# Five of 64 large stores split into strided transfers meant to relieve one DMA engine

## Chip, cores, metric

One core of a Trainium2 chip. The batches of runs were on different chips (0, 3, 5, 6, 8 and 10 by the record; that of the first pair is not recorded), and each is compared with the kernel before in its own batch. The metric is the device time of one execution in microseconds (us), the median of several runs. Engine names are those of the profile: PE is TensorE, DVE is VectorE, ACT is ScalarE, POOL is GpSimd, SP is SyncE. The profile counts 16 DMA engines for the core and does not number them. Where the texts number engines, the numbers are my names: 7 for the one that the change was to relieve, 15 for a second.

## The reference

Attention of one query row per head, and its gradients, 64 heads (2 x 32), 8192 keys, head size 128, all bf16:

```python
def _fwd_reference(q, k, v):              # q [2,32,1,128], k and v [2,32,8192,128]
    scale = q.shape[-1] ** -0.5
    scores = jnp.einsum("bhqd,bhkd->bhqk", q, k) * scale
    p = _softmax(scores, axis=-1)
    return jnp.einsum("bhqk,bhkd->bhqd", p, v)

def reference(q, k, v, grad_out):
    out, vjp = jax.vjp(_fwd_reference, q, k, v)
    return out, *vjp(grad_out)            # out, dq, dk, dv
```

k and v are read once (268 MB) and dk and dv written once (268 MB); everything else is small.

## The kernel before

The heads are worked on in 32 pairs. A pair's k is one tile of 4 MB in SBUF, 128 partitions of 128 rows of 256 bytes, and its v is another. Six such tiles circulate. The gradient is written over the tile itself, the tile is stored, and then the slot takes the next load:

```python
load_eng = nc.sync
store_eng = nc.gpsimd
pin = tc.keep_in_program_order
# ...
def load(i, w, pieces=(NCH,)):                          # w = 0: k, w = 1: v
    h = pairs_[i]
    t = kvp.tile([P, NT, D], BF16, tag=f"kv{slot_of(i, w)}", name="kvt")   # six slots
    # ...
        pin(load_eng.dma_start(out=t[:, n0:n1, :], in_=src[:, n0:n1, :]))  # L93
# ...
def outer(i, w, c, ends):
    # ... DVE writes the gradient of chunk c over the tile ...
    if c + 1 in ends:                                   # ends is whole: one store per tile
        at = ends.index(c + 1)
        b0, b1 = (ends[at - 1] if at else 0) * CH, (c + 1) * CH
        dst = (dv_v if w else dk_v)[i]
        pin(store_eng.dma_start(out=dst[:, b0:b1, :], in_=h.tile[w][:, b0:b1, :]))   # L446
```

A load of a slot waits for the store of what the slot held. In the trace each store's semaphore gets 16 increments, and the load is issued about 0.1 us after the 16th (at 194.77, 215.03, 235.12 and 255.31 us for stores whose 16th came at 194.7, 214.9, 235.1 and 255.2 us). The program gives the DMAs of the store queue eight semaphores in turn (the trace shows eight, 111 to 118), so a transfer is issued only when the one eight before it has landed.

## Time and profile before

| | before |
|---|---|
| median of 3 runs | 1308.88 us (1304.53 to 1310.17) |
| span of the profiled run, mean TensorE clock | 1310.5 us, 0.923 |
| bytes moved, mean rate | 539.58 MB, 412 GB/s |
| wait of the load queue for stores | 1188.3 us |

The page of the kernel before: span, busy tenths in 40 equal slices, mean rate of each slice, and the transfers by size with their median time from issue to landing.

```profile
span 1310.5 us, 41375 instructions
...
POOL 0000000000000000000000000000000000000000
...
DMA  9999999999999999999999999999999999999968
GB/s 399 429 374 429 427 429 427 429 428 428 427 424 417 429 422 421 413 415 418 414 413 412 411 417 420 413 417 419 403 421 411 421 408 414 425 404 423 414 257 348
DMA packets 19933, 539.58 MB, mean 412 GB/s; under 512 B 2480, under 2 KB 2480, under 8 KB 2992
...
out_dram<-kvt POOLq DMA_DIRECT2D x62, 4096.0 KB, 40.2
```

The DMA engines are busy throughout, and POOL, which issues the stores, has almost nothing to do.

The longest waits of the load queue's sequencer in the kernel before (total us, times, longest us):

```profile
SPq L93 <- DMA out_dram<-kvt: 1188.3, 58, 59.9
```

Nearly every load waits for a store. The same kernel in five stretches (window, length, busy time of PE, PE weight loads, DVE, ACT and POOL, TensorE clock, DMA share, GB/s):

```profile
100.00:300.00 200.00, 186.52 (x3208) 138.71 (x3205) 143.22 (x260) 165.92 (x111) 5.84 (x11) 0.96 1.00 429
300.00:500.00 200.00, 178.81 (x2965) 132.45 (x2965) 131.24 (x240) 152.30 (x100) 5.32 (x10) 0.92 1.00 424
500.00:700.00 200.00, 176.98 (x2906) 130.43 (x2904) 128.14 (x233) 149.38 (x98) 4.78 (x9) 0.91 1.00 415
700.00:900.00 200.00, 178.59 (x2961) 131.92 (x2958) 131.18 (x238) 152.32 (x100) 5.32 (x10) 0.92 1.00 415
900.00:1060.00 160.00, 138.72 (x2276) 102.60 (x2275) 102.56 (x185) 116.89 (x75) 4.25 (x8) 0.90 1.00 415
```

The rate falls from 429 to 415 GB/s while the DMA share stays 1.00. The semaphores hint at why. I take the 16 increments of a store to come from one engine each. That is an inference: the store queue has 1088 packets of 4 bytes for 68 transfers, 16 for each. Some store landings read from the trace, in us:

```
before   1st    12th    13th    16th
       187.7   191.2   191.9   194.7
       205.9   210.7   211.2   214.9     <- the store that the change splits first
       225.5   231.6   232.1   235.1
       243.7   251.0   251.4   255.2
```

From 100 us on, the last increments follow each other every 20.2 us on average. The last increment is about 2 to 3 us behind the first at 100 us, and 16 to 22 us behind it from 320 us on, with a gap of its own behind the fifteenth of mostly 6 to 11 us. I read this as one engine that lags: the others run ahead for the first 300 us, at 429 GB/s, and then wait for it. The profile does not say which engine it is.

The change assumes that the rows of partitions 28-31 and 60-63 are the slow engine's, and that its transfers hand them to other engines.

### The profile page before, as it was taken

What the parts mean: (1) busy time and instruction counts of PE and PEld (TensorE: products, weight loads), DVE (VectorE), ACT (ScalarE), POOL (GpSimd) and SP (SyncE); (2) the same over time, 40 slices, a digit from 0 to 9 for tenths busy, and PEclk for the clock granted to TensorE, in tenths of its full rate; (3) what the DMA queues carried; (4) which work ended last, traced back from release to release, by engine and by line L of the source; (5) the groups of instructions that cost most, each with busy time, mean ns of one, the idle gap of its engine ahead of it and who ended that gap; (6) DMA issues with size and microseconds to landing.
All of it is one profiled execution on the core that took longest, in us unless ns stands there. A gap on an engine that the chain in (4) does not pass through costs nothing.

```text
span 1310.5 us, 41375 instructions
## 1 busy us (share of the span) xinstructions
PE 1147.5 (88%) x19108; PEld 849.1 (65%) x19108; DVE 850.5 (65%) x1551; ACT 984.3 (75%) x641; POOL 37.4 (3%) x76
## 2 busy tenths in 40 slices
PE   5999998898988988989889898898998988888894
PEld 4777766676766666666666676666666666666661
DVE  0677875766766767657676675665766757566666
ACT  5999987876877877778777787777876878777770
POOL 0000000000000000000000000000000000000000
PEclk9999998998989989889898898988988989888896
DMA  9999999999999999999999999999999999999968
GB/s 399 429 374 429 427 429 427 429 428 428 427 424 417 429 422 421 413 415 418 414 413 412 411 417 420 413 417 419 403 421 411 421 408 414 425 404 423 414 257 348
DMA packets 19933, 539.58 MB, mean 412 GB/s; under 512 B 2480, under 2 KB 2480, under 8 KB 2992
## 3 DMA queue, kind: packets, MB, share of 16 engines
q1 hardware_dynamic: 9968, 268.51, 49.5%
q0 software_dynamic: 9792, 268.44, 48.2%
q8 instruction: 149, 2.44, 0.7%
q14 instruction: 24, 0.20, 0.0%
HBM read 268.47 MB, written 268.47 MB: 410 GB/s over the span
## 4 chain that ended last, share of the span: by engine, by line
issue 78%; DMA 14%; PE 3%; POOL 2%; DVE 1%; SPq 0%; POOLq 0%; ACT 0%; DVEq 0%; ACTq 0%
DMA kvt<-in_v_dram 11%; DMA out_dram<-kvt 3%; POOL out_dram L446 2%; PE tp L183 1%; DVE kvt L432 1%; PE acc L376 1%; PE dpw L194 1%; POOLq L446 0%; PE sw L194 0%; ACT ev L185 0%; DVE sel L399 0%; SPq L93 0%; SPq L100 0%; PE sw L222 0%; PE acc L413 0%
## 5 line engine op out<-in xcount | busy, mean ns | idle before, releaser
L185 ACT COPY ev<-tp 128x2048 bf16<-128x2048 bf16 x512 | 954.0, 1865 | 293.6 <-PE tp L183 276.1
L183 PE MATMUL tp<-ident_bf,kvt 128*128 128x128 bf16 x8192 | 585.3, 229 | 127.3 <-DMA kvt<-in_k_dram 76.8
L432 DVE TENSOR_TENSOR kvt<-qb,pair 128x2048 bf16<-128x2048 bf16 x512 | 615.3, 1219 | 49.6 <-PE acc L376 46.7
L183 PEld LDWEIGHTS <-kvt 128*128 128x128 bf16 x8192 | 505.1, 103 | 137.2 <-DMA kvt<-in_k_dram 79.1
L194 PEld LDWEIGHTS <-ev 128*128 128x128 bf16 x8192 | 239.9, 96 | 218.0 <-issue 135.4
L376 PE MATMUL acc<-kvt,E_pad 128*64 128x512 bf16 x1024 | 173.1, 421 | 0.0
L376 PE MATMUL acc<-kvt,dS_pad 128*64 128x512 bf16 x1024 | 169.4, 416 | 1.0 <-DVE dS_pad L362 1.0
L194 PE MATMUL sw<-qdT,ev 128*128 128x2 bf16 x4096 | 142.0, 164 | 2.2 <-ACT ev L185 2.2
L194 PE MATMUL dpw<-qdT,ev 128*128 128x2 bf16 x4096 | 142.2, 164 | 1.0 <-ACT ev L185 1.0
L270 DVE CUSTOM_DVE_ANT_0 junk<-E_f,dpw 64x128 bf16<-64x128 f32 x64 | 18.3, 285 | 144.1 <-PE dpw L194 143.7
L207 DVE TENSOR_REDUCE mp<-sw 64x1 f32<-64x128 f32 x64 | 18.5, 289 | 108.5 <-PE sw L194 108.1
L446 POOL DMA_DIRECT2D out_dram<-kvt x68 | 36.3, 534 | 1261.7 <-DVE kvt L432 632.9
L399 DVE SCALAR_TENSOR_TENSOR sel<-acc,diag,sel 128x128 f32<-128x128 f32 x192 | 67.3, 351 | 6.8
L376 PEld LDWEIGHTS <-dS_pad 128*64 128x64 bf16 x1024 | 38.2, 112 | 29.4 <-issue 6.3
L376 PEld LDWEIGHTS <-E_pad 128*64 128x64 bf16 x1024 | 37.7, 112 | 26.8 <-issue 6.5
L262 DVE CAST E_pad<-E_f 64x128 bf16<-64x128 f32 x64 | 15.3, 239 | 48.5 <-ACT E_f L252 48.5
L413 PE MATMUL acc<-par,sel 128*128 128x2 f32 x128 | 22.0, 241 | 8.0 <-DVE sel L399 8.0
L176 DVE CAST qb<-dpw 128x128 bf16<-128x128 f32 x64 | 18.2, 284 | 13.4 <-PE dpw L167 13.4
L413 PEld LDWEIGHTS acc<-par,sel 128*128 128x128 f32 x128 | 19.7, 195 | 9.5 <-DVE sel L399 9.5
L340 DVE TENSOR_SCALAR negdelta<-dpw,rl 128x1 f32<-128x1 f32 x32 | 7.0, 218 | 27.0 <-PE dpw L300 27.0
L252 ACT ACTIVATE E_f<-sw,negm 64x128 f32<-64x128 f32 x64 | 23.2, 362 | 1.6
L352 DVE SCALAR_TENSOR_TENSOR dSu<-dpw,negdelta,E_f 64x128 f32<-64x128 f32 x64 | 22.4, 350 | 2.1
(49 smaller groups left out, 230.1 us busy)
## 6 DMA issues: line engine op xcount, KB each, us to landing
out_dram<-kvt POOLq DMA_DIRECT2D x62, 4096.0 KB, 40.2
kvt<-in_v_dram SPq DMA_DIRECT2D x32, 4096.0 KB, 27.8
kvt<-in_k_dram SPq DMA_DIRECT2D x31, 4096.0 KB, 27.9
out_dram<-kvt POOLq DMA_DIRECT2D x3, 2048.0 KB, 8.7
kvt<-in_k_dram SPq DMA_DIRECT2D x1, 2048.0 KB, 11.5
kvt<-in_k_dram SPq DMA_DIRECT2D x2, 512.0 KB, 4.5
kvt<-in_k_dram SPq DMA_DIRECT2D x1, 1024.0 KB, 6.9
out_dram<-kvt POOLq DMA_DIRECT2D x1, 1024.0 KB, 7.6
```

The costliest lines, as they stand in the source:

```text
L183: pin(nc.tensor.transpose(tp[:, t, :], src[:, c * CH + t, :], ident_bf[:]))
L185: pin(nc.scalar.copy(out=ev[:], in_=tp[:]))
L194: nc.tensor.matmul(dst[:, c * CH + t, :], lhsT=ev[:, t, :], rhs=qdT[:, w, GH * i : GH * (i + 1)], start=True, stop=True,)
L207: pin(nc.vector.reduce_max(out=h.mp[hs], in_=h.s[hs, :, g], axis=AX.X))
L252: nc.scalar.activation(out=h.E_f[hs], in_=h.s[hs, :, g], func=ACT.Exp, bias=h.negm[hs], scale=scale, accum_out=h.ld[hs, g : g + 1],)
L270: nc.vector.tensor_tensor_reduce(out=junk[hs], in0=h.E_f[hs], in1=h.dp[hs, :, g], scale=1.0, scalar=0.0, op0=ALU.mult, op1=ALU.add, accum_ ...
L352: nc.vector.scalar_tensor_tensor(out=dSu[hs], in0=h.dp[hs, :, g], scalar=negdelta[hs], in1=h.E_f[hs], op0=ALU.add, op1=ALU.mult,)
L376: nc.tensor.matmul(h.acc[w][g : g + CW, :], lhsT=wts[:, n0 * GH : n0 * GH + CW], rhs=rows[:, n0 : n0 + QT, :].rearrange("p n d -> p (n d)" ...
L399: nc.vector.scalar_tensor_tensor(out=h.sel[:], in0=block, scalar=diag[:, b : b + 1], in1=h.sel[:], op0=ALU.mult, op1=ALU.add,)
L413: nc.tensor.matmul(h.acc[w][:, 0:GH], lhsT=h.sel[:], rhs=par[:], start=True, stop=True)
L432: nc.vector.tensor_tensor(out=h.tile[w][:, n0 : n0 + CH, :].rearrange("p n (e t) -> p n e t", t=2), in0=h.qb[w][:] .rearrange("p (e t) -> ...
L446: pin(store_eng.dma_start(out=dst[:, b0:b1, :], in_=h.tile[w][:, b0:b1, :]))
```

## The change

For the k stores of pairs 3, 9, 15, 21 and 27, write partitions 28-31 and 60-63, but for one row of 256 bytes per partition, in two transfers of their own, and the rest in 24 strided ones. One store becomes these 26 transfers and eight calls with mode `reset_dge_cursor`:

```diff
-            pin(store_eng.dma_start(out=dst[:, b0:b1, :], in_=h.tile[w][:, b0:b1, :]))
+            if w == 0 and i % 6 == 3 and ends is whole:
+                spread(dst, h.tile[w], b0, b0 + NT // 1)
+                b0 += NT // 1
+            if b0 < b1:
+                pin(store_eng.dma_start(out=dst[:, b0:b1, :], in_=h.tile[w][:, b0:b1, :]))
+
+    def spread(dst, t, b0, b1):
+
+        def put(parts, r0, r1, pieces=1, eng=store_eng):
+            pin(
+                eng.dma_start(
+                    out=dst[parts, r0:r1, :],
+                    in_=t[parts, r0:r1, :],
+                    max_dma_last_dim=(r1 - r0) * D * 2 // pieces,
+                )
+            )
+
+        for j in (0, 1, 2, 3, 32, 33, 34, 35):
+            pin(store_eng.inc_swdge_sem([], [], mode="reset_dge_cursor"))
+            put(slice(j, j + 29, 4), b0, b0 + 1, 2)
+            put(slice(64 + j, 64 + j + 29, 4), b0, b1, 2)
+            put(slice(j, j + 25, 4), b0 + 1, b1)
+        for p0 in (28, 60):
+            put(slice(p0, p0 + 4), b0 + 1, b1)
```

Below, "piece" is one of these transfers and "tail" one of the last two, of partitions 28-31 and of 60-63.

## The prediction

> **What bounds the kernel now.** DMA traffic. The page shows 539.58 MB at 412 GB/s; stretches from 100 to 1060 us show a DMA share of 1.00. In the sequencer's own waits, loads wait 1188.3 us for stores to land: six 4 MB tiles circulate, and a load needs its slot's store to have landed [...].
>
> One engine is slower than the other 15. Each DMA's semaphore gets 16 increments[...]. For the stores landing near 74 to 114 us they lie 2 to 3 us apart. From about 320 us the last comes 16 to 22 us after the first, mostly 6 to 11 us after the fifteenth. Stretches show 429 GB/s at 100 to 300 us and 415 from 500 on: fifteen engines first run ahead, then wait for the slow one. Full-rate packets of 32 KB take 1213 ns; 429 GB/s is 1222 ns per packet and engine; the slow engine's landings, 20.14 us per tile (16 packets), are 1259 ns. 37 ns x 1024 packets = 38 us. The others' idle time hides in load packets stretched past 1213 ns (about 20 us per 50 us, summed over 16 engines, after 500 us) and in the last load, which the first engine finishes at 1242 us and the last at 1261.
>
> The profile does not say which engine it is. [...] the change takes it to be 7.
>
> **What the change does.** In the k stores of pairs 3, 9, 15, 21, 27, partitions 28-31 and 60-63 [...] are written by two small transfers [...]. [...] Perfectly balanced: about 1310 - 36 = 1274 us.
>
> **What it costs.** One issue becomes 26, plus 8 resets. POOL issues take 0.53 us each, so some 15 to 20 us per spread store; POOL is 97% free. Worse: stores share eight semaphores, and each transfer waits for the one eight before it. The eighth piece thus waits until the previous whole store has landed, about 20 us; then at most eight pieces (under three rows per engine) are in flight. A store on an idle queue took about 4 us from issue to first packet, so pieces run at half to all of the rate they need. The next store is issued some 15 us late. My estimate: 1.5 to 7.5 us of idle per spread store on the fast engines, giving back 8 to 37 of the 36 us. Compute is unchanged.
>
> **Prediction.** 1288 us, range 1274 to 1308; faster by over 2%: 0.30, within 2%: 0.66, slower: 0.04.
>
> **Signs.** Landings of ordinary stores stay within about 10 us of each other throughout; GB/s stays near 425 after 400 us; stretched load packets become rarer; POOL waits about 20 us for store landings in each spread store, and DMA dips after it. The last load lands near 1240, not 1261.
>
> **What would make it wrong.** The slow engine is 15: time unchanged or worse, landings spread as before. The eight-semaphore window starves the stores more than estimated: dips of 10 us or more, no gain. Or pieces land so quickly that nearly the whole 36 us comes.

The sum came to 1310 - 36 + 8 to 37 = 1282 to 1311 us, of which 1288 was given. The relief, 36 us, is an estimate for perfect balance: the 38 us of excess (37 ns x 1024) less its sixteenth. That the change would bring it was assumed.

## The result, and the profile after

| | before | after |
|---|---|---|
| median | 1308.76 us (4 runs) | 1385.02 us (4 runs, 1382.32 to 1388.35) |
| ratio | | 1.059, 95% interval 1.0556 to 1.0623: slower |
| profiled span, clock | 1310.5 us, 0.923 | 1380.5 us, 0.906 |

A ratio here is the mean time of one kernel's runs over the mean of the other's in the same rounds, so not quite the ratio of the medians quoted.

The page of the kernel after, the same lines:

```profile
span 1380.5 us, 41575 instructions
...
POOL 0000012000001300000022000001300000111000
...
DMA  9999998899999898999999899999998999989888
GB/s 404 426 377 426 430 408 304 365 411 425 423 429 420 305 380 362 416 422 425 425 378 324 373 416 416 428 427 401 312 395 363 415 426 424 426 335 338 359 344 352
DMA packets 24014, 539.61 MB, mean 391 GB/s; under 512 B 6240, under 2 KB 6240, under 8 KB 6752
...
out_dram<-kvt POOLq DMA_DIRECT2D x57, 4096.0 KB, 38.6
...
out_dram<-kvt POOLq DMA_DIRECT2D x40, 256.0 KB, 7.1
out_dram<-kvt POOLq DMA_DIRECT2D x40, 222.2 KB, 6.5
...
out_dram<-kvt POOLq DMA_DIRECT2D x10, 127.0 KB, 16.4
```

The bytes are the same and the rate is lower. There are five dips to 304-335 GB/s, one for each spread store. The last line is the surprise: the ten tails carry 127 KB each and take 16.4 us to land, longer than pieces of twice the size.

The waits of the load queue in the kernel after:

```profile
SPq L93 <- DMA out_dram<-kvt: 1264.9, 65, 59.9
```

This wait grew by 1264.9 - 1188.3 = 76.6 us, and the span of the same two profiled runs by 1380.5 - 1310.5 = 70.0 us (the medians by 76.3 us). The loss lies in late stores.

POOL in the kernel after, around the first spread store (start, length, line, and in brackets its idle time before and what ended it). Line 456 is a piece, line 450 an ordinary store:

```profile
175.58 4.01 POOL L456 DMA_DIRECT2D out_dram<-kvt  x7 [18.39 <-DVE sel L393]
194.83 0.55 POOL L456 DMA_DIRECT2D out_dram<-kvt  x1 [15.25 <-DMA out_dram<-kvt]
197.28 0.54 POOL L456 DMA_DIRECT2D out_dram<-kvt  x1 [1.90 <-DMA out_dram<-kvt]
198.72 0.60 POOL L456 DMA_DIRECT2D out_dram<-kvt  x1 [0.91 <-DMA out_dram<-kvt]
201.09 0.55 POOL L456 DMA_DIRECT2D out_dram<-kvt  x1 [1.77 <-DMA out_dram<-kvt]
203.53 0.54 POOL L456 DMA_DIRECT2D out_dram<-kvt  x1 [1.89 <-DMA out_dram<-kvt]
207.83 0.61 POOL L456 DMA_DIRECT2D out_dram<-kvt  x1 [3.76 <-DMA out_dram<-kvt]
211.65 7.14 POOL L456 DMA_DIRECT2D out_dram<-kvt  x13 [3.21 <-DMA out_dram<-kvt]
218.78 1.11 POOL L450 DMA_DIRECT2D out_dram<-kvt  x2
```

The same stretch in the kernel before:

```profile
173.93 0.53 POOL L446 DMA_DIRECT2D out_dram<-kvt  x1 [17.76 <-DVE sel L393]
193.37 0.53 POOL L446 DMA_DIRECT2D out_dram<-kvt  x1 [18.91 <-DVE kvt L432]
215.29 0.53 POOL L446 DMA_DIRECT2D out_dram<-kvt  x1 [21.38 <-DVE sel L393]
```

Seven pieces are issued at once. The eighth waits 15.25 us, until the previous whole store has landed at 194.5 us, and the next ones come one by one as earlier pieces land (a piece that lands at 197.0 us is followed by an issue at 197.28 us); the last 13 are issued without a wait. The next ordinary store is issued at 218.78 us instead of 193.37 us, 25.4 us late. The prediction said this (with 15 us), and it is not the larger part of the loss. That part is seen in the landings:

```
after    1st    12th    13th    16th
       187.6   191.9   192.1   194.5    the ordinary store before
       ...
       218.7   220.0   220.0   221.2    last of the 24 pieces before the tails
       219.6   221.4   227.7   230.3    tail of partitions 28-31
       219.9   221.6   237.4   239.0    tail of partitions 60-63
       230.1   239.5   250.9   256.2    the next ordinary store
       239.8   257.5   270.7   275.6
       256.9   276.9   290.7   295.6
```

The pieces end at 221.2 us, 6.3 us after the 214.9 us at which the whole store had landed before. Then the tails take another 17.8 us, on four engines going by their four late increments, while twelve of the second tail's 16 are in by 221.6 us, and eleven of the next store's by 232.5 us. The second tail comes after the first, it seems on the same four engines: its four packets start at 227.41, 229.26, 229.44 and 229.89 us, and those of the first end at 227.32, 228.96, 229.37 and 229.82 us. In that next store twelve increments arrive by 239.5 us and the other four from 250.9 us on. Each of the 40 packets of the tails (32512 bytes) took 7.3 to 9.7 us; the median of the other 280 packets of that size was 1.2 us.

The store ends 24.1 us late. The next stores then come every 19.5 us or so, the pace of packets of 1.213 us (16 of them are 19.4 us), as if the four engines worked through their backlog, and eleven stores later 14.7 us of the delay is left (451.3 us against 436.6 us). Each of the five spread stores leaves 13 to 15 us in this way; together they are the 70 us of the profiled runs.

### The profile page after: what moved, and what is told of

It is laid out like the page before. It is cut to its first block, busy times and chain, and to the rows that moved or that the text cites. A ratio compares the mean times of both kernels' runs of the same rounds, so it can differ in the third digit from the quotient of the medians.

```text
span 1380.5 us, 41575 instructions
## 1 busy us (share of the span) xinstructions
PE 1117.3 (81%) x19108; PEld 830.6 (60%) x19108; DVE 851.5 (62%) x1551; ACT 984.2 (71%) x641; POOL 107.1 (8%) x201
## 4 chain that ended last, share of the span: by engine, by line
DMA 45%; issue 29%; PE 17%; POOL 4%; DVE 3%; ACT 2%; SPq 0%; POOLq 0%; ACTq 0%; DVEq 0%
DMA out_dram<-kvt 24%; DMA kvt<-in_v_dram 20%; PE tp L183 8%; PE acc L376 4%; POOL out_dram L456 3%; PE dpw L194 2%; DVE kvt L432 2%; PE sw L194 2%; ACT ev L185 1%; DMA qd_nat<-in_q_dram 1%; POOL out_dram L450 1%; ACT E_f L252 0%; PE sw L222 0%; PE dpw L313 0%; PE dpw L300 0%
## 5 line engine op out<-in xcount | busy, mean ns | idle before, releaser
L183 PE MATMUL tp<-ident_bf,kvt 128*128 128x128 bf16 x8192 | 568.0, 225 | 225.2 <-DMA kvt<-in_v_dram 190.9
L183 PEld LDWEIGHTS <-kvt 128*128 128x128 bf16 x8192 | 489.1, 101 | 234.9 <-DMA kvt<-in_v_dram 192.9
L376 PE MATMUL acc<-kvt,E_pad 128*64 128x512 bf16 x1024 | 163.1, 400 | 0.0
L450 POOL DMA_DIRECT2D out_dram<-kvt x63 | 33.8, 538 | 1019.1 <-DVE sel L393 580.3
L456 POOL DMA_DIRECT2D out_dram<-kvt x130 | 72.3, 560 | 242.5 <-DMA out_dram<-kvt 134.4
## 6 DMA issues: line engine op xcount, KB each, us to landing
out_dram<-kvt POOLq DMA_DIRECT2D x10, 127.0 KB, 16.4
```

What stands on the lines that cost most here:

```text
L183: pin(nc.tensor.transpose(tp[:, t, :], src[:, c * CH + t, :], ident_bf[:]))
L376: nc.tensor.matmul(h.acc[w][g : g + CW, :], lhsT=wts[:, n0 * GH : n0 * GH + CW], rhs=rows[:, n0 : n0 + QT, :].rearrange("p n d -> p (n d)" ...
L456: eng.dma_start(out=dst[parts, r0:r1, :], in_=t[parts, r0:r1, :], max_dma_last_dim=(r1 - r0) * D * 2 // pieces,)
```

## The experiments

The theory after reading the two traces was: the tails cost most of the loss, the eight semaphores the rest, and the relief gave nothing. The rivals were that the relief did come and the pieces cost all the more, and that the engine meant to be relieved was slow but spread stores hid it. Each experiment is an edit of the changed kernel, or of the kernel before where said.

### 1. tail_dropped: the change without its tails (wrong result)

```diff
-        for p0 in (28, 60):
-            put(slice(p0, p0 + 4), b0 + 1, b1)
```

> Wrong result on purpose: in the five spread stores partitions 28-31 and 60-63 are not written (except their first 256 bytes); the other 24 pieces are unchanged. Theory T (the two 4-partition transfers, whose 32.5 KB packets took about 9.2 us instead of 1.2 us, cost the time by holding four engines some 19 us): 1275 to 1300 us, below the kernel before. Theory W (the window of eight semaphores starves the stores while the 24 pieces are issued): 1365 to 1385 us, as the changed kernel. If both matter, the difference to the changed kernel is T's part and the rest W's; each spread store's cost in the changed kernel was 24.6 us (landing of the spread store, 239.0 against 214.9 us).

Measured: 1321.80 us, before in the same batch 1309.60 us, ratio 1.0101 (1.0086 to 1.0116). The two tails, 6% of the bytes of a spread store (254 of 4096 KB), cost 1385.02 - 1321.80 = 63 us, or 12.6 us per spread store.

### 2. home_rows: the same pieces with the tails' rows in them, no tails

```diff
-            put(slice(j, j + 25, 4), b0 + 1, b1)
-        for p0 in (28, 60):
-            put(slice(p0, p0 + 4), b0 + 1, b1)
+            put(slice(j, j + 29, 4), b0 + 1, b1, 2)
```

> The lower pieces take 8 partitions each, [...] the two 4-partition transfers are gone: no relief, no tail, only 24 pieces and 8 resets in five stores. Theory T: 1305 to 1325 us (as before, plus at most 3 us per spread store). Theory W: 1385 us or more, since the relief is lost as well. In both, the ordinary stores away from the spread ones should again land every 20.3 us and not every 19.4 us as in the changed kernel, if it is engine 7 that is slow; if they stay at 19.4 us the relief was not what made them faster.

Measured: 1322.67 us, ratio 1.0111 (1.0084 to 1.0138). Splitting alone costs 13 us, 2.6 us per spread store. This kernel writes all rows, tail_dropped leaves out those of partitions 28-31 and 60-63 in the five stores (but for 256 bytes per partition), and they differ by 0.9 us, inside both intervals. Not having to write these rows is worth nothing that these runs can see.

### 3. tail_four_ports: four-partition transfers that are not neighbours

In home_rows, the groups j = 3 and j = 35 are written by two transfers of four partitions, each four apart:

```diff
+            if j in (3, 35):
+                for p0 in (j, j + 16):
+                    put(slice(p0, p0 + 13, 4), b0 + 1, b1)
+            else:
+                put(slice(j, j + 29, 4), b0 + 1, b1, 2)
```

> [...] the groups j=3 and j=35 are written by two 4-partition transfers each, of partitions 4 apart. So there are four transfers of 4 partitions instead of two, with the same 32.5 KB packets, but their partitions are 4 apart and not neighbours. If 4-partition transfers are slow as such (split into small pieces, or few engines), their packets take about 9.2 us again and the time is near 1400 us. If the neighbouring partitions are what is slow (four engines reading the same place), the packets take 1.2 to 1.5 us and the time equals that of home_rows within 15 us.

Measured: 1326.03 us, ratio 1.014 (1.0117 to 1.0163). These transfers on the page, to be held against the tails' 16.4 us:

```profile
out_dram<-kvt POOLq DMA_DIRECT2D x20, 127.0 KB, 4.2
```

The 80 packets of 32512 bytes had a median of 1.2 us, and one took over 2.5 us. A transfer of four partitions is not slow as such; what sets the tails apart is that their four partitions are neighbours.

### 4. home_halves: home_rows with its large pieces cut in two

Each group's two large transfers are cut in halves, so 40 pieces instead of 24:

```diff
+            for r0, r1 in ((b0, b0 + 64), (b0 + 64, b1)):
+                put(slice(64 + j, 64 + j + 29, 4), r0, r1, 2)
+                put(slice(j, j + 29, 4), max(r0, b0 + 1), r1, 2)
```

> home_rows with every large piece cut in two along the row: 40 pieces per spread store instead of 24[...]. If the 13 us that home_rows loses come from the window of eight pieces in flight (2.6 us per spread store), the eight now hold half as many bytes and the loss should at least double: 1335 to 1365 us. If they come from something that does not depend on the number of pieces (the wait of about 15 us for the previous store, the resets, the order of engines), it stays at 1318 to 1328 us.

Measured: 1357.55 us, before 1306.30 us, ratio 1.0397 (1.038 to 1.0414), so 51 us instead of 13 us. Same bytes, pieces half as large. The time is in the range that I gave for the window of eight in flight, but the trace gives another cause. POOL's line of pieces in home_rows and in home_halves (count, busy us and mean ns, idle us before and the part of it that ended with a landing):

```profile
L456 POOL DMA_DIRECT2D out_dram<-kvt x120 | 67.1, 561 | 254.9 <-DMA out_dram<-kvt 147.0
L456 POOL DMA_DIRECT2D out_dram<-kvt x200 | 111.1, 558 | 252.4 <-DMA out_dram<-kvt 141.8
```

The waits for landings did not grow, 147.0 and 141.8 us. The time POOL spends issuing did, by 44 us, against 38 us of added run time. At the first spread store of home_halves, 27 of the 40 pieces were issued in one go, in 15.07 us, without a wait for any landing. A group of five pieces carries 512 KB in 5 x 558 ns, an estimated 188 GB/s, less than half of what the engines move between the dips. So the added cost is POOL's serial issuing, not the window. How the 13 us of home_rows divide between the two was not measured. The page of this run, slices of the rate:

```profile
GB/s 402 427 377 427 427 412 259 424 431 431 426 430 429 268 380 431 432 429 429 429 381 230 419 429 430 429 426 428 261 381 430 430 430 430 429 387 245 418 430 365
```

and of home_rows:

```profile
GB/s 397 426 371 430 431 412 351 419 429 430 430 429 430 337 401 429 430 432 429 428 405 344 426 426 434 428 430 429 292 404 432 432 427 429 429 408 328 427 394 351
```

The dips are deeper, and the stretches between them are as good. Both kernels keep about 430 GB/s (426 to 434) between the dips, above the 415 of the kernel before at the same times. That is no gain: the landings of each spread store are together within some 2 us, so after each standstill the fifteen faster engines may run ahead of the slow one once more.

### 5. probe_neighbours: extra transfers of neighbours and others (kernel before, look only)

Behind each of the same five k stores, one small extra transfer to spare memory:

```diff
+    # ... the loop that issues them is left out here and below
+    probes = {
+        3: (slice(28, 32), slice(0, 4)),
+        9: (slice(28, 32), slice(8, 24, 4)),
+        15: (slice(0, 16, 4), slice(32, 36)),
+        21: (slice(30, 34), slice(40, 44)),
+        27: (slice(28, 30), slice(48, 50)),
+    }
```

> The kernel before, with one extra small transfer to a scratch tensor after each of the five stores, each row 32.5 KB: (a) partitions 28-31 to neighbouring rows of memory, as in the changed kernel: 9 us per packet expected; (b) partitions 28-31 to rows 128 KB apart; (c) partitions 0, 4, 8, 12 to neighbouring rows; (d) partitions 30-33 to neighbouring rows; (e) partitions 28 and 29 alone. If the reading side (four engines reading one place of SBUF) is the cause: (b) 9 us, (c) 1.2 us, (d) and (e) half of (a) or less. If the writing side (neighbouring rows in memory) is: (b) 1.2 us, (c) 9 us, (d) 9 us.

Measured: 1307.86 us. Partitions 28-31 to neighbouring memory rows took 1204, 1722, 3440 and 3933 ns per packet, to rows 128 KB apart 1204, 1204, 2202 and 2219 ns; partitions 0, 4, 8, 12 took 1204 ns each, 30-33 also; 28-29 took 2902 and 2874 ns. The packets hardly overlapped in time, so this separated too little. It was repeated with more load.

### 6. probe_rows: each extra transfer three times in a row (kernel before, look only)

```diff
+    probes = {                                # partitions, first memory row, step between rows
+        3: (slice(28, 32), 0, 1),
+        9: (slice(28, 32), 12, 4),
+        15: (slice(0, 16, 4), 60, 1),
+        21: (slice(28, 30), 72, 8),
+        27: (slice(28, 31, 2), 76, 8),
+    }
```

> As probe_neighbours, but each extra transfer three times in a row so that its engines do overlap: (a) partitions 28-31 to neighbouring rows; (b) 28-31 to rows 128 KB apart; (c) partitions 0, 4, 8, 12 to neighbouring rows; (d) 28 and 29 to rows 256 KB apart; (e) 28 and 30 to rows 256 KB apart. Reading side the cause: (a) and (b) both 3.5 to 9.5 us per packet, (c) 1.2 us, (d) about 2.9 us as 28 and 29 took before. Writing side the cause: (b), (d), (e) 1.2 us and (c) as slow as (a). (e) tells whether two of four neighbouring partitions, not side by side, still collide. Time within 2% of the kernel before.

Measured: 1328.74 us. Packets of 32512 bytes: partitions 28-31 to neighbouring rows 4178 to 8498 ns, to rows 128 KB apart 2582 to 8509 ns; partitions 0, 4, 8, 12 twelve times 1204 ns; 28 and 29 1212 to 4086 ns; 28 and 30 1206 to 3961 ns. So the slow packets go with the partitions that are read together, and the memory rows do not matter.

Whether only neighbours slow each other, the last probe tests.

### 7. probe_ports: what do the readers share? (kernel before, look only)

```diff
+        3: (slice(28, 61, 32), 0, 1),         # (a) 28, 60: 32 apart
+        9: (slice(28, 93, 64), 12, 1),        # (b) 28, 92: 64 apart
+        15: (slice(28, 45, 16), 24, 1),       # (c) 28, 44: 16 apart
+        21: (slice(28, 30), 36, 1),           # (d) 28, 29: neighbours
+        27: (slice(28, 125, 32), 48, 1),      # (e) 28, 60, 92, 124: 32 apart
```

> Five probes behind five k stores, each a transfer written three times in a row to spare memory, one packet of 32512 bytes per partition [...]. Their packets should take 1.2 us when nothing collides, and 1.2 to 4.1 us when two engines read one place (28 and 29, 28 and 30 in probe_rows). What is one place? [...] Theory G: only the group of four neighbouring partitions. Then (a), (b), (c) and (e) are all at 1.2 us, and (d) alone is slow.

Measured: 1305.61 us. Packets: 28 with 60: 1204 to 1742 ns; 28 with 92: 1204 to 1209 ns; 28 with 44: 1204 ns but for one packet of 2161 ns; 28 with 29: 1204 to 5442 ns; 28, 60, 92 and 124: 1204 to 7281 ns, five of twelve above 3.3 us. The last is not what theory G allows: no two of these four are in one group of four neighbours, so readers further apart can slow each other too. The run is not clean: 28 with 60 was hardly slower, and one packet of 28 and 44 was. In the trace, packets of 28 and 60 overlapped in time only once, by 0.7 us, and these two were the slowest of the six (1513 and 1742 ns); two packets of 28 and 92 that overlapped by 1.0 us took 1204 ns each. Theory G alone does not hold; the rival theory described a larger shared place that no run shows. What the readers share stays open.

### 8. Which engine is slow: hw_stores (kernel before, stores from another queue)

```diff
-    store_eng = nc.gpsimd
+    store_eng = nc.scalar
```

> The kernel before with all stores issued from the scalar engine's hardware queue instead of GpSimd, nothing else. If the one slow engine is slow because of software descriptors (its store packets took about 1340 ns where the others took 1213), the lag of 16 to 22 us between the first and the last of a store's sixteen landings goes away and the time falls to 1275 to 1295 us, less what the scalar engine loses by waiting in order for the stores' inputs (1 us per store would be hidden). If an engine is slow for another reason, the lag stays and the time is 1305 to 1320 us.

Measured: 1308.52 us, ratio 1.0003 (0.9981 to 1.0025). From 600 us on the last increment still came 25 to 28 us after the first, while the fifteenth came 8 us after it at first and 2 to 6 us from 700 us on. The page lists these stores as hardware_dynamic (268.44 MB) and those of the kernel before as software_dynamic, so the software queue is not what makes the lag. Which engine lagged in this run (chip 0) was not looked for.

### 9. mark_loads, mark_hw_stores and mark_low: small loads behind large ones (kernel before, look only)

A tiny load of k rows is queued behind each 4 MB load or store. The thought was that it lands late only if it takes part in what is behind, so that markers of different k, compared, tell where the lag is. How the rows of a marker go to engines, no run shows. What the expectations say of markers and engines (engine 15 in mark_loads, the smallest k in mark_low) was my reading before the runs and rests on that too.

```diff
+    # ... the calls are left out; mark_loads: after every load; mark_hw_stores: after every store
+    def mark(eng):
+        for m, t in zip((7, 8, 15), marks):
+            pin(eng.dma_start(out=t[:m], in_=q_rows[:m]))
```

> The kernel before, with three tiny marker loads (7, 8 and 15 partitions of 256 bytes) behind every 4 MB load, on the same hardware queue. [...] If engine 15 is slow, all three markers land together, several us before the last increment of the 4 MB load ahead of them. [...] Time within 1% of the kernel before.

Measured: 1358.85 us; the markers themselves cost time. Still, where a load's last increment was late (15th at 780.9 us, last at 788.8 us), the marker of 7 was late with it (791.2 us). So seven rows already met what was late.

> The same markers behind every store of hw_stores, on the stores' hardware queue, where the last of the sixteen landings came 25 us after the first and over 20 us after the fifteenth from 600 us on, so the answer should be plainer. [...]

Measured: 1435.41 us, 128.8 us over the kernel before in the same batch (1306.60 us). Too disturbed to answer; inconclusive.

mark_low uses fewer and smaller markers, of 1, 2, 3 after some loads and of 4, 5, 6 after others:

```diff
         if (i := at(O1 + NCH)) is not None and i + 3 < NP:
             load(i + 3, 0)
+            if i % 4 == 1:
+                mark(1, 2, 3)
         if (i := at(O0 + NCH)) is not None and i + 3 < NP:
             load(i + 3, 1)
+            if i % 4 == 3:
+                mark(4, 5, 6)
```

> The markers behind the loads [...] (the 7-marker landed 2 to 3 us after the load's last increment, the 15-marker with it). Now fewer markers, of 1, 2, 3 partitions behind seven of the loads and 4, 5, 6 behind seven others. The slow engine is the smallest k whose marker lands with or after the load's last increment while the next smaller one landed several us earlier[...]

Measured: 1311.71 us. Where a load had its 15th increment at 1039.3 us and its last at 1059.9 us, the marker of 4 landed at 1041.7 us, that of 5 at 1062.4 us. In another, 566.6 and 574.9 us: marker of 4 at 569.1 us, of 5 at 577.5 us. Markers of 1, 2 and 3 were early, also behind loads with a late last increment (marker of 3 at 788.2 us, load at 795.8 us). In all five places from 530 us on the marker of 4 was early and that of 5 late. I read this as one slow engine that the fifth row brings in (engine 4 in the texts), an inference.

### 10. extra4, extra5, extra8: four, five and eight packets more per k store (kernel before)

Behind each of 31 k stores, one row of 32512 bytes from each of 4, 5 or 8 partitions four apart goes to spare memory. Had one of the engines of the first four packets been the slow one, about 38 us more were expected of extra4 already, by an estimate: 31 packets of 1.21 us.

```diff
+            if w == 0 and ends is whole:
+                pin(
+                    store_eng.dma_start(
+                        out=scratch[EXTRA * i : EXTRA * (i + 1), 1:b1, :],
+                        in_=h.tile[w][0 : 4 * EXTRA : 4, 1:b1, :],
+                        max_dma_last_dim=(b1 - 1) * D * 2,
+                    )
+                )
```

> The kernel before, with one small extra transfer behind each of 31 k stores: partitions 0, 4, 8, 12, one row of 32.5 KB each, to a scratch tensor[...]. Each of these engines gets 31 x 1.21 = 38 us more to do. If engine 4 alone sets the pace and these four have some 38 us of slack over the run, the time rises by 0 to 10 us: 1306 to 1320 us. [...]

Measured: 1305.20 us, ratio 0.998 (0.9963 to 0.9997).

> The same with partition 16 added[...]. If engine 4 is the slow one[...], the time rises by 30 to 42 us over the kernel before: 1338 to 1352 us. [...]

Measured: 1349.87 us, ratio 1.0322 (1.0307 to 1.0337).

> The same with partitions 20, 24 and 28 added[...]. If engine 4 is the slow one and 7 is not, this is within 8 us of extra5. [...]

Measured: 1346.52 us, ratio 1.0299 (1.0284 to 1.0315).

Four extra packets per store cost nothing, the fifth 42 us, and three more nothing on top. At the slow engine's 1259 ns per packet, 31 packets are an estimated 39 us. So the fifth packet, of partition 16, seems to fall on the engine that sets the pace, and the others fall on engines with slack. This is the same answer as that of the markers, by another way and on another chip (6; mark_low was on chip 8).

### 11. drop4, drop4_pool, drop_none_pool: would relief of the right engine have paid?

I took the slow engine's rows to be those of partitions 16-19 and 48-51. No run shows this; extra5 bears on partition 16 alone, in a small extra transfer. Pieces as in home_rows, but the lower ones separate these rows, so that they can be left out (wrong result; one row of 256 bytes per partition is still written) or written:

```diff
+            put(slice(j, j + 17, 4), b0, b0 + 1, 2)
+            put(slice(j + 20, j + 29, 4), b0, b1, 2)
+            put(slice(64 + j, 64 + j + 29, 4), b0, b1, 2)
+            put(slice(j, j + 13, 4), b0 + 1, b1, 1, nc.scalar)   # drop4: partition j + 16 left out
+            put(slice(j, j + 13, 4), b0 + 1, b1)                 # drop4_pool instead
+            put(slice(j, j + 17, 4), b0 + 1, b1)                 # drop_none_pool instead
```

> Wrong result on purpose: [...] Relief of the right engine: 5 x 8 x 1.26 = 50 us less for it. Theory that relief pays when the engine is the right one: 1285 to 1305 us, clearly under tail_dropped's 1322. Theory that the stall of the spread store makes all engines wait anyway, so that no relief given inside it counts: 1315 to 1330 us.

Measured: 1365.12 us, ratio 1.0444 (1.042 to 1.0469). ACT issues of the first spread store in drop4:

```profile
175.25 38.84 ACTq L456 DMA_DIRECT2D out_dram<-kvt  x8
```

Its eight pieces hold up ACT's queue for 38.84 us, and the compute waits: PE's weight loads for ACT 293.8 us in all and up to 41.2 us at once, against 69.2 and 0.9 us in the kernel before. The run says nothing about relief. With all pieces on POOL:

> Wrong result on purpose: [...] To be read against drop_none_pool, the same pieces with nothing left out. Theory A, relief of the right engine pays: the slow engine has 5 x 32 packets of 1.26 us = about 100 us less to do, more than its whole excess over the others (36 to 40 us), so this run should be 15 to 40 us below drop_none_pool. Theory B, the standstill of each spread store already lets the slow engine catch up, so that nothing is left for relief to give at that moment: within 5 us of drop_none_pool.

Measured: 1328.64 us, ratio 1.0165 (1.0148 to 1.0182).

> The control of drop4_pool: the same 32 pieces per spread store[...]. Right result. Window theory: 32 pieces of which at most eight are in flight cost more than home_rows' 24 (13 us) and less than home_halves' 40 (51 us): 1325 to 1350 us.

Measured: 1341.68 us, ratio 1.0258 (1.0242 to 1.0273). POOL's waits for landings in drop4_pool:

```profile
POOL out_dram L456 <- DMA out_dram<-kvt: 130.5, 40, 14.0
```

and in drop_none_pool:

```profile
POOL out_dram L456 <- DMA out_dram<-kvt: 143.6, 41, 16.2
```

A store has 128 packets of 32 KB, eight per engine if they are shared evenly, so if the rows left out are the slow engine's, it has an estimated 5 x 8 x 1.26 = 50 us less to do (the 100 us in my expectation was a miscount). Leaving them out brings 13 us. My theory A asked for 15 to 40 us and theory B for under 5 us, so neither was right: leaving out these rows pays (leaving out partitions 28-31 and 60-63 in tail_dropped brought 0.9 us), but about a third of the 36 us that I had credited to the change, and less than the 35 us that these 32 pieces cost over the kernel before (1341.68 - 1307.04). The 13 us also stand as the fall in POOL's waits, from 143.6 to 130.5 us; that is agreement, not proof that they are the same 13 us.

### 12. skim4_a: a try at a faster version (kernel before)

The last 24 rows of every whole k store, in three transfers (5, 120 and 3 partitions) meant to relieve the slow engine:

```diff
+            skim = 24 if w == 0 and ends is whole else 0
+            e0 = b1 - skim
+            pin(store_eng.dma_start(out=dst[:, b0:e0, :], in_=h.tile[w][:, b0:e0, :]))
+            if skim:
+                pin(store_eng.inc_swdge_sem([], [], mode="reset_dge_cursor"))
+                for p0, p1 in ((0, 5), (8, 128), (5, 8)):
+                    pin(
+                        store_eng.dma_start(
+                            out=dst[p0:p1, e0:b1, :],
+                            in_=h.tile[w][p0:p1, e0:b1, :],
+                            max_dma_last_dim=skim * D * 2 // 2,
+                        )
+                    )
```

> A try at a faster version: every whole k store leaves the last 24 of 128 rows per partition to three later transfers, of 5, 120 and 3 partitions[...]. [...] the stores have only four transfers each, so the window of eight is no limit. If the relief is all that happens: 1270 to 1290 us. If reads of the same group of four SBUF partitions by two engines at once slow them (probe_rows: 1.2 us for 32 KB becomes 1.2 to 4 us for two), the gain is lost: 1300 to 1400 us.

Measured: 1315.72 us, before 1307.04 us, ratio 1.0062 (1.0045 to 1.0078). No gain, and a loss of 8.7 us. The relief that I had counted on rested on which engines these transfers take. No run shows that, so why it lost was not shown. None of the versions tried is a useful gain over the kernel before.

## Why the prediction was wrong

It gave 1288 us, 1274 to 1308, and put 4% on a loss of over 2%. The time was 1385.02 us. Its sum was 1310 - 36 for relief + 8 to 37 for the pieces. Measured:

| term | predicted | measured | by |
|---|---|---|---|
| relief | -36 us | none seen | home_rows and tail_dropped, 0.9 us apart |
| pieces, eight in flight | +8 to +37 us | +13 us | home_rows; home_halves points to POOL's issuing |
| the two tails | not in the sum | +63 us | after and tail_dropped |

- **"One engine is slower than the other 15"** agrees with extra4 and extra5 (-3 and +42 us).
- **"the change takes it to be 7"** is the step that failed first. It stood for the rows of partitions 28-31 and 60-63, and leaving them out brought 0.9 us. What was late came in with the fifth row or packet, on the two chips where it was looked for closely (8, marker of 5; 6, extra5 with +42 us); on a third (10) a marker of seven rows was already late. The lag stayed with hardware-issued stores (25 to 28 us from first to last increment). The prediction named engine 15 as the way it could be wrong, and no other; it gave "time unchanged or worse" for that case.
- **"are written by two small transfers"** is the step that cost 63 us. I counted the tails' bytes and not what they share: eight packets read from neighbouring partitions four at a time, at 7.3 to 9.7 us each instead of 1.2 us. Nothing in the trace of before could show it: its stores are of 128 partitions, with a median of 1.213 us per packet of 32 KB, and no transfer of four neighbouring partitions is in it.
- **The window of eight semaphores**: the wait was as predicted ("The eighth piece thus waits until the previous whole store has landed": 15.25 us at the first spread store), and the loss of 2.6 us per spread store lies in my range of 1.5 to 7.5. That is in part luck. I had ranked POOL's issue time below the window ("POOL is 97% free. Worse: ..."), and when pieces were added it was the issue time that grew (67.1 to 111.1 us) and not the waits for landings (147.0 to 141.8 us).
- **The signs**: the dips came. The landings did not stay within 10 us of each other, and four engines, not one, were late after each spread store.
- **Would the right engine have saved it?** In this form no gain was seen: drop4_pool, without the rows of partitions 16-19 and 48-51 and without tails, is still 1.65% slower than the kernel before. With home_rows' 24 pieces (13 us) the same 13 us would about break even, an estimate that was not run. What a form without standstill could get was not measured.

Why the engine of the fifth packet is slow stays open, and so is whether it is the engine or the place in SBUF that it reads, since no run shows which engine moves which partitions. The trace of the kernel before has one hint: from 500 to 1060 us, 172 of 3532 store packets took 1.27 to 1.40 us instead of 1.213, nearly half of them 2.4 to 2.7 us apart, as if they were one engine's, in turn with loads of 1.213 us per packet. Their excess is about 0.67 us per tile, most of the 0.8 us by which the 20.2 us per tile exceed 16 x 1.213 us. So the lag may arise in that engine's stores, an inference and not shown. Also open is what exactly the readers of neighbouring partitions share, and how much 28 and 60, whose packets hardly overlapped in probe_ports, slow each other.

## What to carry to other kernels

Before moving work off a slow DMA engine, find out which rows bring it in, by adding packets to the stores a few at a time: here the time rose by 42 us with the fifth packet per store, and not with the four before it or the three after it. When a store is split into small transfers, choose each one's partitions so that they are not neighbours; partitions four apart kept 1.2 us per packet here, neighbours took 7.3 to 9.7 us. Many small transfers on one queue cost their issue time (0.56 us each on POOL here) and wait for what may be in flight (15.25 us for the eighth piece here), so halving the pieces can cost more than the relief is worth.
